# A held order of some 2000 operations made anew, with one copy and one product on other engines

## The chip, the cores and the metric

The kernel runs on one core of one Trainium2 chip. Its time is the device time of one execution in microseconds (us). Engines are named as the profile names them: PE is TensorE (PEld its weight loads), DVE is VectorE, ACT is ScalarE, POOL is GpSimd, SP is SyncE, which here only issues transfers and loads registers.

## The reference

Attention of 4 batches, 8 heads, 768 positions and 64 dimensions, with a sink of 4 positions and a window of 128, is followed by a mixture of experts in which each of the 3072 tokens goes to one of 8 experts:

```python
keep = (pos[None, :] < n_sink) | ((rel >= 0) & (rel < window))
scores = np.where(keep, q @ k.T / sqrt(D), -1e9)
a = np.exp(scores - scores.max(-1)); a /= a.sum(-1) + 1e-09
x = (a @ v) as (3072, 512)
e_idx = np.argmax(x @ w_gate, axis=1)
gate_w = softmax(x @ w_gate)[token, e_idx]
eom = sigmoid(x @ w_output_gate)
for e in range(8):
    out[e_idx == e] = gate_w * eom[:, e] * (np.maximum(x_e @ w1[e], 0) @ w2[e])
```

## The kernel before

**A planner.** The kernel does not issue its work as the loops come. Each operation is recorded with `pl.op(engine, duration, function, reads, writes, at=due time)`, and `Plan.order()` makes a list schedule from it: it steps through the five engines, starts on each the operation that can begin earliest by the assumed durations, and among those that can begin within a few tens of ns of it takes the one with the lowest due time. The order that comes out is then held on every engine. So a table of due times (`AT`), the assumed durations (`dve`, `act`, `gps`, literal numbers) and the assumed delays (`LAG`, `RATE`, `LAND`) decide, before anything runs, which operation stands behind which in each engine's queue.

**Attention** is 16 pairs of heads, 4 to a batch. `pair` issues for a pair: scaling q on POOL (L1060, three parts), scores on PE (L1076), fold of the window and row maximum on DVE (L1083 to L1088), exps on ACT (L1092), transposes of the exps on PE (L1112) in three groups j = 0, 1, 2, the copy of each group out of PSUM (ACT L1117, for j = 1 DVE L1119), masks of the copy on POOL (L281, tiles f and g), the product with v on PE (L1170, L1182), the gate's product (L1192), its copy lgT on ACT (L1196) and transposes (L1202), the weighing lw on DVE (L1206), and the division of the output by the sums, x, on DVE (L1235, after PE L1232). x is stored to a table xd in memory.

**Routing** follows a batch. `gate_route` takes maximum and chosen expert on DVE (L411 to L426), counts with small matmuls on PE (L442, L444), finds each token's place (L454 to L481), builds ohrow on DVE (L487) and three parts of rhs (L495, two on POOL and the third on DVE), and sorts with a product on PE (L507). After batches 1 and 2 `rank_experts` (L549 to L571) and `early_table` choose two experts each for the early slots 0 to 3. After batch 3 `final_table` (L653 to L740, DVE alone) picks 13 more slots, one after another, and after each four picks works out a chunk of token indices (L691 to L710, then L538 to L540).

**The experts** are 17 slots. A slot gathers tokens from xd by indirect transfers on POOL (L765, tile xg), transposes them on PE (L825) into a high part xh (ACT L828) and a low part xl (DVE L830), multiplies by w1 (m1, L944; slot 0 plain, L925) into two PSUM buffers named s, takes the relu as hh (ACT L856) and hl (DVE L859), multiplies by w2 (m2, L982), scales the result, y (ACT L838), by the factor sc that was copied out of the gathered row (ACT L848), and writes it by an indirect transfer on POOL (L841). Raw weights come in by SP (L797) into four buffers and are split into a high part (ACT L800) and a low part (DVE L804).

Of the kernel before, what the change touches and what calls it, by code (L numbers as in the profile page):

```python
# [18 lines left out]
P = 128  # L19
# [29 lines left out]
SLOT0, STEP, PLAIN = 172000, 20000, 1  # L49
# [13 lines left out]
class Plan:  # L63

    LAG = {"PE": 180, "ACT": 40, "DVE": 40, "POOL": 60, "SP": 0, "X": 0}
    NEAR = {"PE": 60, "ACT": 60, "DVE": 60, "POOL": 100, "SP": 100, "X": 0}
    SWITCH = {"row": 200}
    RATE, LAND = 0.35, 2000
# [18 lines left out]
    def op(self, eng, took, fn, r=(), w=(), at=0, busy=None, mode=None, size=0, behind=(), chain=None, hold=()):  # L87
# [23 lines left out]
        if isinstance(at, tuple):  # L111
            cls, at = at, at[0] + sum(AT[x] for x in at[1:])
        self.ops.append({"cls": cls, "eng": eng, "took": took, "busy": took if busy is None else busy, "fn": fn, "deps": deps - {i},
                         "uses": uses, "at": at, "mode": mode, "size": size, "chain": chain})
        return i

    def order(self):
# [13 lines left out]

        def room(fam, n):
# [11 lines left out]
        def start_of(i):  # L144
            o = ops[i]
            t = max(free[o["eng"]], earliest[i])
            if o["mode"] is not None and o["mode"] != mode:
                t += self.SWITCH.get(o["mode"], 150)
            elif o["mode"] is not None and t > free["PE"] + 50:
                t += 60  # L150
# [12 lines left out]
        while len(out) < len(ops):
            best = None
            for e, xs in ready.items():
# [3 lines left out]
                lim = min(ts)[0] + self.NEAR[e]  # L169
# [1342 lines left out]
```

## Time and profile before

| | |
|---|---|
| time, median of 3 runs | 607.68 us (604.41 to 612.07) |
| the profiled execution | 606.5 us; its span 604.7 us |
| granted TensorE clock, mean | 0.953 of full speed |
| busy: PE, DVE, ACT, POOL | 516.4, 357.1, 274.4, 190.9 us |
| attention and routing of three batches | 0 to about 230 us |
| slots 0 and 1, final table | about 230 to 290 us |
| the other slots | about 290 us to the end |

The three stretches overlap: an early slot is prepared while the last pairs run. PE holds most of the span, so the places where PE stands idle are what to look for, each with the instruction that ended it. A row of the timeline gives in brackets how long its engine was idle ahead of it, and what released it.

### The profile page before, as it was taken

The numbers are of one execution on the slowest core, as the hardware profiler recorded it, in microseconds if no ns is written. First come the engines' busy times: TensorE is split into PE (matmuls) and PEld (weight loads), VectorE is DVE, ScalarE is ACT, GpSimd is POOL, SyncE is SP. The second block draws the span as 40 slices with busy tenths as digits, with TensorE's granted clock in tenths as the row PEclk, the third lists the DMA queues.
The fourth block names the chain that finished last, engine by engine and source line by source line (L and its number), as shares of the span: only waits on it lengthen the run. The fifth ranks groups of instructions, "written<-read, shape, count | busy, mean of one in ns | idle before, by whom it ended". The sixth has DMA issues, their size and how long they took to land. (4 is left out here: it accounts for less than half of the span.)

```text
span 604.7 us, 10373 instructions
## 1 busy us (share of the span) xinstructions
PE 516.4 (85%) x3480; PEld 401.3 (66%) x3480; DVE 357.1 (59%) x822; ACT 274.4 (45%) x725; POOL 190.9 (32%) x292
## 2 busy tenths in 40 slices
PE   4999788888885997875888999999999698989992
PEld 2566555555554783664878788798777586677972
DVE  6776786598668644989762345435546344556420
ACT  4566566445753533434162434515535334356320
POOL 8467574766754410311112121121110302100110
PEclk9799999899998998979798999999999988999998
DMA  7354757389952376545653883636797717968540
GB/s 218 122 138 137 136 143 138 99 173 386 278 135 55 50 174 133 159 155 173 210 194 120 315 311 106 232 120 226 268 337 247 240 41 238 339 236 291 198 164 17
DMA packets 68959, 112.60 MB, mean 186 GB/s; under 512 B 8316, under 2 KB 35200, under 8 KB 68898
## 3 DMA queue, kind: packets, MB, share of 16 engines
q1 hardware_dynamic: 64434, 97.94, 53.5%
q0 software_dynamic: 4464, 13.91, 7.2%
q8 instruction: 30, 0.49, 0.4%
q14 instruction: 31, 0.25, 0.1%
HBM read 98.26 MB, written 13.25 MB: 184 GB/s over the span
## 5 line engine op out<-in xcount | busy, mean ns | idle before, releaser
L1092 ACT ACTIVATE e<-s,nmx 128x132 f32<-128x132 f32 x192 | 69.7, 371 | 56.1 <-DVE nmx L1088 39.9
L1076 PE MATMUL s<-k,q 64*128 64x260 f32 (+1 forms) x384 | 65.1, 431 | 13.2 <-ACT e L1092 6.5
L859 DVE SCALAR_TENSOR_TENSOR hl<-s,hh 128x512 fp32r<-128x512 f32 (+1 forms) x36 | 26.8, 749 | 71.9 <-ACT hh L856 71.9
L841 POOL DMA_INDIRECT out_dram<-y,idx x20 | 21.6, 1079 | 139.7 <-ACT y L838 104.8
L765 POOL DMA_INDIRECT xg<-xd,idx x21 | 22.9, 1091 | 130.0 <-PE tp L825 123.5
L1076 PEld LDWEIGHTS s<-k,q 64*128 64x128 f32 x384 | 34.0, 200 | 31.9 <-ACT e L1092 15.3
L856 ACT ACTIVATE hh<-s 128x512 fp32r<-128x512 f32 (+1 forms) x36 | 23.0, 644 | 68.0 <-PE s L944 66.0
L1085 DVE COPY_PREDICATED s<-maskf,s 128x256 f32<-128x256 int32 x80 | 33.8, 422 | 29.4 <-PE s L1076 25.8
L1060 POOL TENSOR_SCALAR q<-q 128x256 f32<-128x256 f32 x48 | 40.4, 856 | 11.4 <-DMA q<-in_qT_dram 9.0
L1088 DVE TENSOR_REDUCE nmx<-s 128x2 f32<-128x264 f32 x96 | 41.5, 432 | 3.3
L1092 ACT ACTIVATION_READ_ACCUMULATOR e<-s,nmx 128x1 f32 x192 | 38.7, 202 | 0.0
L1112 PE MATMUL tp<-ident,e 128*128 128x128 f32 x192 | 31.7, 291 | 4.2 <-DVE x L1235 2.4
L281 POOL TENSOR_SCALAR_AFFINE_SELECT g<-f 128x512 f32<-128x512 f32 (+1 forms) x48 | 28.4, 592 | 21.0 <-ACT f L1117 10.5
L1112 PEld LDWEIGHTS tp<-ident,e 128*128 128x128 f32 x192 | 21.6, 146 | 13.7 <-issue 3.5
L281 POOL TENSOR_SCALAR_AFFINE_SELECT f<-f 128x512 f32<-128x512 f32 (+1 forms) x48 | 28.6, 595 | 3.3
L830 DVE TENSOR_TENSOR xl<-tp,xh 128x512 fp32r<-128x512 f32 x23 | 15.4, 687 | 23.7 <-ACT xh L828 14.4
L1170 PE MATMUL oA<-f,v 128*64 128x128 f32 x256 | 26.7, 287 | 2.4 <-ACT e L1092 1.6
L838 ACT ACTIVATE y<-oA,sc 128x512 f32<-128x512 f32 (+1 forms) x18 | 11.7, 651 | 32.8 <-PE oA L982 27.2
L848 ACT COPY sc<-xg 128x1 f32<-128x1 f32 x28 | 5.0, 195 | 45.9 <-DMA xg<-xd,idx 28.2
L1235 DVE TENSOR_TENSOR x<-tp,rs 128x512 f32<-128x512 f32 (+1 forms) x32 | 17.6, 550 | 13.7 <-PE tp L1232 7.0
L1117 ACT COPY f<-tp 128x512 f32<-128x512 f32 x32 | 18.7, 586 | 13.3 <-PE tp L1112 12.9
L1232 PE MATMUL tp<-ident,ot 128*128 128x128 f32 x96 | 17.1, 289 | 7.7 <-DVE x L1235 5.6
(537 smaller groups left out, 1555.1 us busy)
## 6 DMA issues: line engine op xcount, KB each, us to landing
raw<-in_w_dram SPq DMA_DIRECT2D x96, 512.0 KB
v<-in_vx_dram SPq DMA_DIRECT2D x16, 384.0 KB
xd<-x SPq DMA_DIRECT2D x16, 384.0 KB
k<-in_kx_dram SPq DMA_DIRECT2D x15, 396.0 KB
q<-in_qT_dram SPq DMA_DIRECT2D x15, 384.0 KB
wa1h<-in_w_dram SPq DMA_DIRECT2D x5, 512.0 KB
wa1l<-in_w_dram SPq DMA_DIRECT2D x5, 512.0 KB
wa2h<-in_w_dram SPq DMA_DIRECT2D x3, 512.0 KB
```

The lines of the kernel that those rows point to most:

```text
L281: nc.gpsimd.affine_select(out=ap, in_=ap if src is None else src, pattern=pattern, compare_op=op, fill=fill, base=base, channel_multiplier=cm)
L765: nc.gpsimd.indirect_dma_start(out=p.get(key), out_offset=None, in_=xd[0:n + 1, :], in_offset=bass.IndirectOffsetOnAxis(ap=ids(), axis=0))
L841: nc.gpsimd.indirect_dma_start(out=where, out_offset=bass.IndirectOffsetOnAxis(ap=ids(), axis=0), in_=p.get(yk)[:, 0:m], in_offset=None, b ...
L856: nc.scalar.activation(out=p.get(hh)[:, :, 0:n], in_=p.get(ps)[:, :, 0:n], func=AF.Relu)
L859: nc.vector.scalar_tensor_tensor(out=p.get(hl)[:, :, 0:n], in0=p.get(ps)[:, :, 0:n], scalar=0.0, in1=p.get(hh)[:, :, 0:n].bitcast(F32), op ...
L1060: nc.gpsimd.tensor_scalar(out=c, in0=c, scalar1=SCALE, scalar2=None, op0=ALU.mult)
L1076: nc.tensor.matmul(out=get(s)[:, a, o0:P + CW], lhsT=get(q)[r, t * P:(t + 1) * P], rhs=get(k)[r, k0:k0 + P + CW - o0], start=True, stop=True)
L1085: nc.vector.copy_predicated(out=both[:, :, 4:CW], mask=bc(maski[:, 1, 4:CW], 1, 2), data=z[:, :, 0:P])
L1088: nc.vector.tensor_reduce(out=get(nmx)[:, t, :], in_=both, axis=AX.X, op=ALU.max, negate=True)
L1092: nc.scalar.activation(out=get(e)[:, t, a, :], in_=get(s)[:, a, P:P + CW], func=AF.Exp, bias=get(nmx)[:, t, a:a + 1], scale=1.0, accum_out ...
L1112: nc.tensor.transpose(out=get(tp)[:, i, :], in_=get(e)[:, 2 * j + i // 2, i % 2, 4:CW], identity=ident)
L1170: nc.tensor.matmul(out=o, lhsT=v_[:, kt, r], rhs=src[:, kt, a, :], start=t == kt == 0 or t == kt + 1 == 4, stop=False, skip_group_check=True)
```

## The change

It replaces the due times and the assumed durations and delays, and so the order on all five engines. Beside that it moves five things: the copies of group j = 1 go from DVE to ACT (16 instructions), the third part of rhs goes from DVE to POOL (4 instructions), the nine small sums that make `unit_of` on POOL become an operation of the plan, `final_table` gets a clock of due times of its own in place of the one that it shared with `gate_route`, and the first product of slot 0 is issued in two halves with other operations behind which it must stand. A cache in the planner makes it quicker and changes no order.

```diff
-SLOT0, STEP, PLAIN = 172000, 20000, 1
+SOFT = 1810
+SLOT0, STEP, PLAIN, FSTEP = 182180, 20000, 1, 800
 AT = {
-    "load": -15884, "v": 16617, "vs": 25612, "sinkv": 22184, "scale0": -9065, "scale1": -12038, "scale2": -3093,
+    "load": -19780, "v": 10768, "vs": 163198, "sinkv": -13952, "scale0": 28418, "scale1": -104693, "scale2": 64567,
...
-    LAG = {"PE": 180, "ACT": 40, "DVE": 40, "POOL": 60, "SP": 0, "X": 0}
+    LAG = {"PE": 260, "ACT": 60, "DVE": 80, "POOL": 55, "SP": 30, "X": 0}
-    RATE, LAND = 0.35, 2000
+    RATE, LAND = 0.39, 2200
...
-                lim = min(ts)[0] + self.NEAR[e]
+                t, i = min(ts)
+                lim = t + max(AT["near"] if e == "PE" else self.NEAR[e], ops[i]["soft"])
...
-def dve(n):
-    return {"took": 160 + 1.045 * n, "busy": 75 + 1.045 * n}
+def dve(n, k=1):
+    return {"took": k * 160 + 1.045 * n, "busy": k * 160 - 85 + 1.045 * n}
...
-                return p.op(eng, fn=fn, r=r, w=w, at=next(clock), **cost)
+                return p.op(eng, fn=fn, r=r, w=w, at=(next(clock), "rt"), **cost)
...
-            for q in (0, 2):
-                v(gps(512, 2.5), expand(nc.gpsimd, q), r=["oh2", "ohj"], w=[("rhs", q)], eng="POOL")
-            v(dve(768), e4, r=["jf"], w=["oh"])
-            v(dve(700), expand(nc.vector, 4), r=["oh2", "ohj"], w=[("rhs", 4)])
+            for q in (0, 2, 4):
+                v({"took": 1490, "busy": 1460}, expand(nc.gpsimd, q), r=["oh2", "ohj"], w=[("rhs", q)], eng="POOL")
+            v(dve(850), e4, r=["jf"], w=["oh"])
...
+        def units_of():
+            for q, z in enumerate(SIZES):
+                if z > 1:
+                    u = unit_of[:, q, 0:z // 2]
+                    nc.gpsimd.tensor_tensor(out=u, in0=u, in1=upp.broadcast_to([P, z // 2]), op=ALU.add)
+
+        pl.op("POOL", 1500, units_of, w=["unit_of"], at=60000)
...
-        def final_table(v):
+        def final_table(p):
+            clock = iter(range(SLOT0, SLOT0 + 1000 * FSTEP, FSTEP))
+            def v(cost, fn, r=(), w=()):
+                return p.op("DVE", fn=fn, r=r, w=w, at=(next(clock), "ft"), **cost)
...
-                    if j != 1:
-                        nc.scalar.copy(out=dst, in_=get(tp))
-                    else:
-                        nc.vector.tensor_copy(out=dst, in_=get(tp))
+                    nc.scalar.copy(out=get(f)[:, two].rearrange("p t a r -> p (t a) r"), in_=get(tp))
```

What the new order does is seen at three places. Names with a number are one buffer each.

DVE, at the end of the final table: the last steps of the table (`nrem`, `more_i`), the low part xl of slot 2's tokens and the low parts of its weights. Before:

```order
L737 TENSOR_REDUCE nrem<-rem 128x1
L738 CAST nrem_i<-nrem 128x1
L739 TENSOR_TENSOR nrem<-nrem,special 128x1
L740 CAST more_i<-nrem 128x1
L830 TENSOR_TENSOR xl_3498<-tp_3407,xh_3432 128x4x128
L830 TENSOR_TENSOR xl_3498<-tp_3419,xh_3432 128x4x128
L804 TENSOR_TENSOR wb2l<-raw_3371,wb2h 128x1024
```

Now the same xl (L867) stands between the sixth and the seventh pick, behind the table's first chunk (`idx`) alone:

```order
L747 SCALAR_TENSOR_TENSOR idx<-idx,upp 128x12
L713 SCALAR_TENSOR_TENSOR key<-units,less 128x8
L714 TENSOR_REDUCE top<-key 128x1
L715 TENSOR_SCALAR who<-key,top 128x8
L867 TENSOR_TENSOR xl_3384<-tp_3332,xh_3352 128x4x128
L719 SCALAR_TENSOR_TENSOR units<-who,units 128x8
L719 SCALAR_TENSOR_TENSOR less<-who,less 128x8
L719 SCALAR_TENSOR_TENSOR off<-who,off 128x8
L867 TENSOR_TENSOR xl_3384<-tp_3340,xh_3352 128x4x128
```

Slot 2's xl has moved from behind the table's four chunks to behind the first of them; the four hl of slot 1, which stood among the first chunks, now stand ahead of the first pick and behind the eight low parts of slot 1's weights (wc0l to wa3l), and the count of batch 3 on PE has moved from the middle of slot 0's second product to behind slot 1's first.

ACT, at the end of the last pair: the copies ot of its output, the factor sc of slot 3's first gather and the last pair's lgT. Before:

```order
L1186 COPY ot_2924<-oA 128x512
L1187 COPY ot_2924<-oB 128x256
L828 CAST xh_2896<-tp_2919 128x4x128
L848 COPY sc_2945<-xg_2889 128x1
L1196 COPY lgT_2954<-oB 96x256
L848 COPY sc_2973<-xg_2937 128x1
```

Now:

```order
L1216 COPY ot_2934<-oA 128x512
L1217 COPY ot_2934<-oB 128x256
L865 CAST xh_2892<-tp_2929 128x4x128
L1226 COPY lgT_2952<-oB 96x256
L885 COPY sc_2969<-xg_2885 128x1
```

lgT has moved ahead of the copy that waits for a gather.

DVE, routing of batch 2 with the ranks of the experts; x is the last output part of that batch but one. Before:

```order
L564 CAST order_i<-od 128x2
L568 COPY had<-taken 128x8
L570 TENSOR_TENSOR taken<-taken,perm 128x8 x2
L571 SCALAR_TENSOR_TENSOR base<-taken,base 128x8
L487 TENSOR_TENSOR ohrow<-io_101,jf 128x768
L495 TENSOR_TENSOR rhs<-oh_141,ohj 128x512
L1235 TENSOR_TENSOR x_2408<-tp_2580,rs_1883 128x256
```

Now that x (`x_2462`) and its weighing stand ahead of the ranks (`u`), and ohrow (L517) is followed by folds of scores (L1122, L1125) and the next pair's x:

```order
L1265 TENSOR_TENSOR x_2462<-tp_2496,rs_2048 128x256
L1236 TENSOR_TENSOR lw_2511<-tp_2491,rs_2048 128x192
L488 TENSOR_TENSOR pos<-pos,ohb 128x48
L489 TENSOR_REDUCE tokpos<-pos 128x6
L579 SCALAR_TENSOR_TENSOR u<-u,io_97 128x8
...
L517 TENSOR_TENSOR ohrow<-io_101,jf 128x768
L1122 COPY_PREDICATED s_2548<-maskf,s_2548 128x2x128
L1125 TENSOR_REDUCE nmx_2352<-s_2548 128x2
L1265 TENSOR_TENSOR x_2572<-tp_2559,rs_2226 128x512
```

The routing's steps have moved from one block to places between the pairs' own steps, and the third rhs is gone from DVE.

## Rows read from the trace of the kernel before

**Rows 1.** The page's first part: busy us of each engine, its share of the span, instructions.

```profile
PE 516.4 (85%) x3480; PEld 401.3 (66%) x3480; DVE 357.1 (59%) x822; ACT 274.4 (45%) x725; POOL 190.9 (32%) x292
```

**Rows 2.** The list of waits of PE, longest first: who waits for whom, us in total, times, longest us.

```profile
PE s L944 <- DVE hl L859: 15.3, 4, 5.9
PE s L944 <- DVE xl L830: 8.9, 2, 8.5
PE s L1076 <- ACT e L1092: 6.5, 11, 1.8
PE tp L1232 <- DVE x L1235: 5.6, 3, 4.8
```

**Rows 3.** PE's timeline: start, duration in us, instruction, count, and in brackets the idle time before it and its releaser. The two rows without brackets follow on the one above them at a few us.

```profile
4.79 1.68 PE L1076 MATMUL s<-k,q 64*128 64x260 f32 x8 [4.79 <-POOL q L1060]
107.27 0.70 PE L1170 MATMUL oB<-g,v 128*64 128x128 f32 x4 [3.87 <-POOL g L281]
194.32 1.12 PE L1232 MATMUL tp<-ident,ot 128*128 128x128 f32 x4 [4.75 <-DVE x L1235]
233.61 2.08 PE L982 MATMUL oB<-wa2h,hh 128*128 128x512 f32 x2 [3.85 <-ACT lgT L1196]
235.80 1.63 PE L982 MATMUL oA<-wa2h,hh 128*128 128x512 f32 x2
238.13 1.02 PE L982 MATMUL oA<-wa2l,hh 128*128 128x512 f32 x2
261.17 0.58 PE L944 MATMUL s<-xh,wb0h 128*128 128x256 f32 x1 [5.92 <-DVE hl L859]
290.24 0.58 PE L944 MATMUL s<-xl,wc3h 128*128 128x256 f32 x1 [8.46 <-DVE xl L830]
330.32 0.39 PE L944 MATMUL s<-xh,wb2h 128*128 128x256 f32 x1 [1.50 <-DVE hl L859]
484.62 0.58 PE L944 MATMUL s<-xh,wc0h 128*128 128x256 f32 x1 [5.48 <-DVE hl L859]
```

**Rows 4.** Busy time in stretches of 10 us: PE, PEld, DVE, ACT, POOL with their counts, then the granted clock, the DMA share and GB/s.

```profile
190.00:200.00 10.00, 5.68 (x36) 4.12 (x38) 7.48 (x18) 2.39 (x13) 3.73 (x6) 0.66 0.15 41
280.00:290.00 10.00, 0.89 (x6) 0.46 (x4) 9.27 (x46) 4.48 (x7) 4.61 (x4) 0.74 0.47 170
```

**Rows 5.** DVE's timeline around the final table: the first step after batch 3's count and the first pick, one of the low parts of weights and the pick behind it, the first chunk from its first step to a pick behind it, an hl of slot 1, xl of slot 2, and two hl of slot 2.

```profile
240.21 0.21 DVE L454 TENSOR_TENSOR pos<-tp,base 128x48 f32<-128x48 f32 x1 [0.56 <-PE tp L444]
243.68 0.16 DVE L676 SCALAR_TENSOR_TENSOR key<-units,less 128x8 f32<-128x8 f32 x1
...
252.04 1.22 DVE L804 TENSOR_TENSOR wc3l<-raw,wc3h 128x1024 fp32r<-128x1024 f32 x1
253.18 0.16 DVE L676 SCALAR_TENSOR_TENSOR key<-units,less 128x8 f32<-128x8 f32 x1
255.08 0.18 DVE L691 TENSOR_TENSOR selq<-who,io 128x32 f32<-128x32 f32 x1
259.89 0.16 DVE L676 SCALAR_TENSOR_TENSOR key<-units,less 128x8 f32<-128x8 f32 x1
260.43 0.68 DVE L859 SCALAR_TENSOR_TENSOR hl<-s,hh 128x512 fp32r<-128x512 f32 x1
288.90 1.28 DVE L830 TENSOR_TENSOR xl<-tp,xh 128x512 fp32r<-128x512 f32 x2
301.69 0.69 DVE L859 SCALAR_TENSOR_TENSOR hl<-s,hh 128x512 fp32r<-128x512 f32 x1 [2.15 <-ACT hh L856]
304.53 0.69 DVE L859 SCALAR_TENSOR_TENSOR hl<-s,hh 128x512 fp32r<-128x512 f32 x1 [2.15 <-ACT hh L856]
```

**Rows 6.** ACT's timeline: copies of sc that wait for a gather, and lgT behind the first of them.

```profile
233.10 0.19 ACT L848 COPY sc<-xg 128x1 f32<-128x1 f32 x1 [5.37 <-DMA xg<-xd,idx_e]
233.20 0.36 ACT L1196 COPY lgT<-oB 96x256 f32<-96x256 f32 x1
328.86 0.19 ACT L848 COPY sc<-xg 128x1 f32<-128x1 f32 x1 [5.13 <-DMA xg<-xd,idx]
483.16 0.19 ACT L848 COPY sc<-xg 128x1 f32<-128x1 f32 x1 [2.77 <-DMA xg<-xd,idx]
```

**Rows 7.** Groups of instructions by line, shapes kept apart: busy us, mean ns of one, idle before them; and the durations of rhs on both engines (minimum, median, maximum in ns).

```profile
L1060 POOL TENSOR_SCALAR q<-q 128x256 f32<-128x256 f32 x48 | 40.4, 856 | 11.4 <-DMA q<-in_qT_dram 9.0
L1117 ACT COPY f<-tp 128x512 f32<-128x512 f32 x32 | 18.7, 586 | 13.3 <-PE tp L1112 12.9
L1119 DVE COPY f<-tp 128x512 f32<-128x512 f32 x16 | 10.7, 670 | 0.0
L495 POOL TENSOR_TENSOR rhs<-oh,ohj x8: 1045/1488/1833, 76.4 to 244.8; 128x512 bf16<-128x512 bf16 x8
L495 DVE TENSOR_TENSOR rhs<-oh,ohj x4: 679/1528/1529, 77.1 to 245.7; 128x512 bf16<-128x512 bf16 x4
```

**Rows 8.** POOL's timeline: a scaling of q that waits for its transfer, with the mask behind it, the nine sums of `unit_of`, and the rhs of batch 2; DVE's timeline: one cast of the ranking in batch 2.

```profile
104.95 1.67 POOL L1060 TENSOR_SCALAR q<-q 128x256 f32<-128x256 f32 x2 [4.94 <-DMA q<-in_qT_dram]
6.34 1.38 POOL L599 TENSOR_TENSOR unit_of<-unit_of,upp 128x3 f32<-128x3 f32 x9
189.62 2.05 POOL L495 TENSOR_TENSOR rhs<-oh,ohj 128x512 bf16<-128x512 bf16 x2 [0.48 <-DVE od L563]
189.65 1.04 DVE L564 CAST order_i<-od 128x2 int32<-128x2 f32 x1
```

More of the change, by code (lines that the diff above doesn't have):

```diff
@@ L85, in get, with op @@
         return x["tile"]
-    def op(self, eng, took, fn, r=(), w=(), at=0, busy=None, mode=None, size=0, behind=(), chain=None, hold=()):
+    def op(self, eng, took, fn, r=(), w=(), at=0, busy=None, mode=None, size=0, behind=(), chain=None, hold=(), land=0, soft=0):
         i = len(self.ops)
@@ L130, in order @@
         end, earliest, out = {}, [0] * len(ops), []
+        stamp = dict.fromkeys(self.fam, 0)
+        opens = {}
+        for fam, xs in self.fam.items():
+            for b in xs:
+                if b["gate"] is not None:
+                    opens.setdefault(b["gate"], set()).add(fam)
+        cached = {}
         def room(fam, n):
@@ L142, in room, with buffers @@
             return xs[:n] if len(xs) >= n else None
[L144 to L150, printed above, removed]
+        def buffers(i):
             need = {}
-            for k in o["uses"]:
+            for k in ops[i]["uses"]:
                 x = self.inst[k]
@@ L920, in slot, with m1 @@
                     ps = new(p, "s", [P, 2, 512])
[L922 to L923 removed]
+                    for j in range(2):
+                        def m1(f0=f0, ps=ps, j=j):
                             for d in range(ND):
@@ L984, in slot @@
                     took = len(tiles) * (f32(512) if plain else 3 * f32r(512))
-                    p.op("PE", fn=m2, r=list(hs[f][0]) + [x for x in w2r[f][:2] if x], w=list(ys.values()), at=at + 11000 + f, **pe(took))
+                    p.op("PE", fn=m2, r=list(hs[f][0]) + [x for x in w2r[f][:2] if x], w=list(ys.values()), at=at + 11000 + f, behind=behind[1:], soft=SOFT if plain else 0, **pe(took))
                 for s in tiles:
@@ L1126, in trans @@
                 pl.op("PE", fn=go, r=[(e, 2 * j), (e, 2 * j + 1)], w=[tp], at=(at, "tr%d" % j), **pe(4 * TR))
-                if j != 1:
-                    pl.op("ACT", fn=copy, r=[tp], w=[(f, j)], at=(at, "tr%d" % j, "trc"), **act(512))
-                else:
-                    pl.op("DVE", fn=copy, r=[tp], w=[(f, j)], at=(at, "tr%d" % j, "trc"), **dve(512))
-                pl.op("POOL", fn=masks, r=[(f, j)], w=[(f, j), (g, j)], at=(at, "tr%d" % j, "mask"), took=n * 600 + 80, busy=n * 600)
+                pl.op("ACT", fn=copy, r=[tp], w=[(f, j)], at=(at, "tr%d" % j, "trc"), **act(512))
+                pl.op("POOL", fn=masks, r=[(f, j)], w=[(f, j), (g, j)], at=(at, "tr%d" % j, "mask"), took=n * 670, busy=n * 650)
             for j in range(3):
@@ L1206, in weigh @@
                 tt(out=get(lw), in0=lr.rearrange("p (t a e) -> p t a e", t=T, a=2), in1=bc(get(rs), 3, 2 * E), op=ALU.mult)
-            eng, name, cost = (nc.gpsimd, "POOL", gps(96)) if p < NP - 2 else (nc.vector, "DVE", dve(96))
+            eng, name, cost = (nc.gpsimd, "POOL", {"took": 390, "busy": 410}) if p < NP - 2 else (nc.vector, "DVE", dve(96))
             def add(a):
@@ L1266, in early @@
             load_reg(k, order_i[0:1, k:k + 1], ("order", r0), at - 14000)
-            slot(pl, k, 4, lambda j, s: idx_e[:, j, k, s:s + 1], ("idx_e", k), xds(done), done * S, at, plain=k < PLAIN, reg=lambda: regs[k], behind=pl.wrote[("s", NP - 1, T - 1)])
+            slot(pl, k, 4, lambda j, s: idx_e[:, j, k, s:s + 1], ("idx_e", k), xds(done), done * S, at, plain=k < PLAIN, reg=lambda: regs[k], behind=before if k == 0 else ())
         def xds(done):
```

132 lines of the change are left out of this document (75 added, 57 removed), and 6 rows, old and new, of the table AT.

## The prediction

> **What bounds the kernel now.** I read the page's first part before anything else: PE is busy for most of the span, no other engine for more than three fifths of it [rows 1]. So the work of PE sets a floor, and what an order can win is PE's idle time and the slow stretches that follow it. The chain of waits is followed back for a few per cent only, so I did not use it, and took the list of PE's waits [rows 2] and PE's timeline [rows 3] in its place. The reader is to see there that a few long waits carry most of it: hl and xl on DVE 24.2 us together, x on DVE 5.6, then lgT, a mask, and the start. Eleven waits for exps come to 6.5, so the short ones are about 0.6 each.
>
> Two things stand behind the long waits. Around the final table DVE is the bound: it is busy 9.27 of 10 us while PE is busy 0.89 [rows 4]. Elsewhere a queue's order is to blame: lgT ran at 233.20, directly behind a copy of sc that had waited 5.37 us for its gather [rows 6], and PE waited 3.85 for lgT [rows 3].
>
> A wait costs more than itself. In the 10 us from 190 the granted clock was 0.66 [rows 4], a mean that must hold stretches at the lower of TensorE's two levels (1.2 against 2.4 GHz). After the wait at 233.61 the next two entries took 2.08 and 1.63 us where the same two matmuls took 1.02 at 238.13 [rows 3]: 1.06 + 0.61 = 1.7 us lost behind a wait of 3.85.
>
> **The change, part by part,** against the profiled execution, 606.5 us (the median of three runs is 607.7, so 1.2 more). A wait that goes is counted at its length, and at 1.7 more where it is long and nothing else will hold PE there.
>
> *lgT of the last pair.* It moves ahead of the copy of sc that waits. Gain 3.85 + 1.7 = **-5.5**. Late next is the last weighing on DVE, which nothing holds. Bounds: -5.5, and 0 if PE then waits for ot instead.
>
> *Routing of batch 2.* DVE takes it as one block, and PE stands 4.75 us for the x behind it [rows 3]. The new order puts that x ahead of the ranks and folds between the steps. 4.75 + 1.7 = 6.45; I take **-6**, since a little of x's own time stays. Bounds -6.5 and 0.
>
> *The final table.* Today PE waits 5.92 for an hl of slot 1 that stands behind the first chunk, and 8.46 for slot 2's xl, which stands behind the whole table [rows 3, 5]; 14.4 together. In the new order count time 0 from the end of batch 3's count. DVE's items up to the end of xl, by pitches from row to row [rows 5]: small steps to the first pick 3.5 less one low part of a weight of 1.14 that stood among them, 2.4; slot 1's last hl 0.7; ohrow about 0.9; three low parts of weights 3.4; a pick 0.8 (between 253.18 and 255.08 lie one pick and one low part), five outside the chunk 3.9; the table's index steps about 0.9; one chunk with its pick 4.8; xl 1.2. Sum 18.2. PE in that time has slot 1's second product. A fourth of a first product is 2.84 (hl to hl in slot 2), a whole one 11.4, the second as many columns; with sort and transposes, some 2, PE is there at 13.4 and waits **4.8**. Two fourths later (23.9) it needs a free s buffer, which slot 2's first hl gives: two picks, three low parts, a chunk, a half pick and the hl are 1.6 + 3.4 + 4.8 + 0.5 + 0.7 = 11.0 on DVE, 29.2, so it waits **5.3** more. Together 10.1 against 14.4, and a short wait for xh goes with it: I take **-5**. Bounds: 0 (DVE's work is the same and only its place differs) and -14.4.
>
> *Copies of sc ahead of hh.* In slot 10 two sc that wait for gathers stand ahead of the first hh; the second ran at 483.16, and PE waited 5.48 [rows 3, 6]. Now the hh is first, and PE has one fourth more to do before it needs the next: **-2.8**. In slot 3 the same at 328.86 cost 1.50 [rows 3, 6] and is put behind the second hh: **-1.5**. From slot 5 on PE, POOL and SP stand nearly as before.
>
> *The start.* The nine sums of `unit_of` take 1.38 us [rows 8] and now stand ahead of the first scaling of q, for which PE waits 4.79 [rows 3]: **+1.4**, with no cover.
>
> *The mask at 107.* POOL's mask stood behind a scaling of q that waited 4.94 for its transfer, and PE 3.87 for the mask [rows 3, 8]. The new order still has scalings between masks; I count half, **-2**, bounds +3.9 and -3.9.
>
> *Copies of f.* Sixteen copies leave DVE, 10.7 us, and come to ACT, 16 x 0.586 = 9.4 [rows 7]. ACT has 45% of the span [rows 1], and a copy fits between its exps; cost 0. Without that cover it would be 9.4. What DVE has free shortens waits for x and folds: **-2** of the short ones, bounds 0 and -5.
>
> *The third rhs.* DVE needed 0.68 for it alone and 1.53 beside POOL's; POOL takes 1.49 [rows 7]. The sort gets it about 1.5 us later. In batch 3 it is done at about 3.7 + 4.5 = 8.2, and PE comes to the sort after six eighths of a product, 8.6: hidden. Batches 0 to 2 lie among pairs. Cost 0; uncovered, 4 x 1.5 = +6. The trace also shows that DVE pays for POOL's work: while two rhs ran on POOL from 189.62, a cast of two elements on DVE took 1.04 us [rows 8]. The Trainium skill, "GPSIMD Engine Reference", opening paragraphs and section 1, speaks against this part of the change: it calls GpSimd the wrong engine for plain elementwise work, about half as fast as VectorE, and says that the two share their access to SBUF when a VectorE instruction has two inputs there. The trace agrees on the speed (1.49 against 0.68). By that rule the move would relieve DVE of little and cost the sort chain its +6.
>
> *New waits.* The order was changed for all five engines, and some pair will wait where none did. The nearest rows are the eleven waits for exps, 0.6 each [rows 2]; eight new ones give **+5**. Bounds: 0, and three of the length seen for x, +14.
>
> Sum: -5.5 - 6 - 5 - 2.8 - 1.5 + 1.4 - 2 - 2 + 5 = -18.4. 606.5 - 18.4 = 588.1, and with the 1.2 between profile and median **589 us**.
>
> **The rivals.**
>
> *The waits only move.* DVE's work up to slot 3 is what it was, and each long wait was one of several nearly as late. Then the table gives 0, batch 2 gives half (-3), the sc copies nothing, and lgT -3.85; with +1.4 and +5 that is 606.5 - 0.5 + 1.2 = 607, and with a part of the forecast's gains some 600. For it: after the new xl the table still stands ahead of slot 2's hl. Against it: DVE had pauses of 2.15 us between slot 2's hl [rows 5], into which the rest of the table can go.
>
> *Everything fits better.* The short waits in attention go too (-5 more on exps and x), no new ones come (-5), and the mask's wait goes whole (-2): 589 - 12 = 577.
>
> *Slower: scalings of q that wait ahead of masks.* POOL takes a later pair's scaling as soon as the order says, also when its transfer is still under way, and the masks behind it hold PE: once before, 3.87 us at 107 [rows 3, 8]. If the new places (two scalings ahead of a pair's last mask in most pairs) meet a late transfer in n pairs, the cost is 3.9 n. From n = 5 the forecast's gain of 18.4 is gone; from n = 8 it is 589 + 31 = 620. Against it: all of POOL's waits for transfers of q came to 9.0 us before [rows 7], 4.94 of it in this one place.
>
> *The third rhs on POOL stretches DVE,* as the cast at 189.65 shows it [rows 8]: up to +6 on the sort chains: 595, or with two lost microseconds elsewhere 597. The 1.04 us cast speaks for it; that the routing now has folds between its steps, against.
>
> **How the numbers follow.** The forecast has 0.48 with 584 to 595, the better fit 0.18, waits that only move 0.19, the stretched DVE 0.08, the late scalings 0.07 (half of it over 2% slower). A measurement here can tell about 2% from no change, 12 us: below 595.5 is faster, above 619.8 slower. Faster: 0.48 + 0.18 + 0.04 of the stretched case, less 0.03 = 0.67. Slower: 0.05, with a little from cases not thought of 0.07. Same: 0.26. The range takes the better fit in to 574 and the moved waits to 607.
>
> **What would show it.** PE's first matmul at about 6.2; no wait of PE for lgT at slot 0's second product; no wait over 2 us for x in batch 2; two waits of some 5 us around slot 2's xl and first hl in place of 5.92 and 8.46; at slot 10 a wait under 3; DVE's busy time down by 10 to 16, ACT's up by 9, POOL's by 6; PE's own busy time down by a few us through less time at the lower clock. The prediction is wrong in its core if PE's idle time around the table stays at 14 us or more, if masks or q appear among PE's longest waits, or if the list shows many new waits of 1 to 2 us in attention.

## The result and the profile after

The changed kernel takes 589.89 us (median of 4 runs, 587.8 to 592.25) against 607.36 us of the kernel before on the same chip: a ratio of 0.971, 95% interval 0.963 to 0.978, faster. The forecast was 589. The profiled execution took 590.1 us, its span is 588.2. All medians leave out executions in a second, slower state: one of h_front's (971.59 us, the other five lie between 594.2 and 602.0), one of h_back's, and a few of the kernel before in the later sessions.

The page's first part of the changed kernel, and PE's list of waits (us in total, times, longest):

```profile
PE 519.1 (88%) x3480; PEld 402.6 (68%) x3480; DVE 346.5 (59%) x802; ACT 280.7 (48%) x741; POOL 193.9 (33%) x296
```

```profile
PE s L981 <- DVE hl L896: 8.8, 6, 3.6
PE s L981 <- DVE xl L867: 6.5, 2, 4.5
PE s L1113 <- POOL q L1097: 6.2, 1, 6.2
PE s L1113 <- ACT e L1129: 6.2, 7, 2.7
PE tp L1175 <- POOL pk L1169: 5.1, 3, 3.3
PE oB L1200 <- POOL g L311: 4.5, 3, 2.5
PE s L981 <- ACT xh L865: 3.4, 2, 2.5
PE tp L472 <- DVE ohb L449: 2.8, 1, 2.8
```

PE stood 604.7 - 516.4 = 88.3 us of the span before [rows 1] and 588.2 - 519.1 = 69.1 now: 19.2 less. Its busy time rose by 2.7 with the same number of instructions, so 16.5 are left. Against [rows 2], hl went from 15.3 to 8.8, xl from 8.9 to 6.5, and x and lgT are gone from the top. New are POOL's pk, ohb behind POOL's logits, and xh. The masks g stand in the list as before (4.8 then, one of 3.87 and a short one; 4.5 now, in three).

PE's timeline of the changed kernel, the rows that answer to [rows 3]:

```profile
6.25 1.68 PE L1113 MATMUL s<-k,q 64*128 64x260 f32 x8 [6.25 <-POOL q L1097]
...
46.66 0.69 PE L1200 MATMUL oB<-g,v 128*64 128x128 f32 x4 [2.50 <-POOL g L311]
71.58 0.20 PE L472 MATMUL tp<-ohb,upper 128*128 128x48 bf16 x1 [2.84 <-DVE ohb L449]
120.42 0.44 PE L1200 MATMUL oB<-g,v 128*64 128x128 f32 x4 [1.78 <-POOL g L311]
138.56 2.06 PE L1113 MATMUL s<-k,q 64*128 64x260 f32 x8 [2.73 <-ACT e L1129]
164.34 0.40 PE L1175 MATMUL tp<-ident,pk 128*40 128x128 f32 x1 [3.29 <-POOL pk L1169]
...
268.06 0.38 PE L981 MATMUL s<-xh,wc3h 128*128 128x256 f32 x1 [2.54 <-ACT xh L865]
272.94 0.58 PE L981 MATMUL s<-xl,wc3h 128*128 128x256 f32 x1 [4.49 <-DVE xl L867]
283.84 0.39 PE L981 MATMUL s<-xh,wc3h 128*128 128x256 f32 x1 [2.46 <-DVE hl L896]
473.91 0.58 PE L981 MATMUL s<-xh,wc0h 128*128 128x256 f32 x1 [3.59 <-DVE hl L896]
```

The wait of 3.87 for a mask at 107 is gone, and four waits for POOL's work of 1.8 to 3.3 us, 10.4 together, stand in attention in its place (ohb at 71.58 is DVE's, and DVE waits there for POOL's lg). POOL's timeline at the first, the third and the fourth of them tells why:

```profile
44.35 0.85 POOL L1097 TENSOR_SCALAR q<-q 128x256 f32<-128x256 f32 x1 [3.44 <-DMA q<-in_qT_dram]
45.17 0.85 POOL L1246 TENSOR_TENSOR lg<-lg,lw 128x96 f32<-128x96 f32 x2
45.97 0.64 POOL L311 TENSOR_SCALAR_AFFINE_SELECT g<-f 128x512 f32<-128x512 f32 x1
...
116.47 1.67 POOL L1097 TENSOR_SCALAR q<-q 128x256 f32<-128x256 f32 x2 [4.57 <-DMA q<-in_qT_dram]
...
160.81 1.68 POOL L1097 TENSOR_SCALAR q<-q 128x256 f32<-128x256 f32 x2 [4.01 <-PE s L1113]
```

A scaling of a later pair's q waits for its transfer, and the sums of logits, masks and packing that PE needs next wait behind it. The second place has the same form: a scaling at 67.20 waited 2.10, lg stands behind it, and DVE waited 2.68 for lg. At the fourth the profile names PE, the last reader of the buffer, as the releaser; whether it or the transfer held the scaling is open. All of POOL's waits for transfers of q came to 16.0 us, against 9.0 before [rows 7].

The fifth new wait, 2.73 for exps at 138.56, has another cause. Batch 1's routing is still one block on DVE, from pos at 131.60 to order_i at 135.98, and the folds and row maxima for those exps stand behind it. That the routing's steps were moved between the pairs' own steps holds for batch 2, not for batch 1.

Each of the four waits for POOL's work has a low clock around it; in the kernel before, the same stretches show 1.00. The windows (columns as in [rows 4]):

```profile
40.00:50.00 10.00, 7.39 (x67) 5.36 (x65) 4.02 (x12) 3.86 (x18) 5.27 (x9) 0.83 0.36 103
70.00:80.00 10.00, 8.42 (x61) 6.19 (x61) 8.45 (x32) 5.24 (x23) 4.12 (x9) 0.66 0.34 91
120.00:130.00 10.00, 9.31 (x53) 5.71 (x55) 6.83 (x22) 5.95 (x24) 6.86 (x12) 0.66 0.43 117
160.00:170.00 10.00, 6.40 (x43) 4.66 (x40) 2.90 (x10) 2.74 (x11) 8.13 (x12) 0.66 1.05 368
```

To place gains, this table (worked out from the starts in the timelines) gives the lead over the kernel before, in us, at four points: the last pair's lw on DVE (236.05 us in the kernel before) and three writes of results on POOL (282.11, 346.58, 594.79). The lower rows are kernels of the experiments. Each row is one execution. In two of the experiments' executions the time was off by 2.3 and 3.8 us ahead of every operation that had been moved, so differences of under 3 us in this table tell nothing by themselves.

| profiled execution | last lw | slot 1's first write | slot 3's first write | last write |
|---|---|---|---|---|
| the changed kernel | 9.3 | 15.4 | 14.7 | 16.5 |
| h_front | 8.3 | 3.6 | 2.7 | 5.7 |
| h_back | 0.0 | 7.6 | 5.8 | 7.4 |
| a_q | 17.5 | 22.3 | 19.8 | 25.3 |
| a_best | 22.6 | 28.4 | 24.8 | 34.6 |
| a_best_tab | 21.1 | 29.1 | 15.8 | 25.1 |

### The profile page after: what moved, and what is told of

It is laid out like the page before. It is cut to its first block, busy times and chain, and to the rows that moved or that the text cites. A ratio compares the mean times of both kernels' runs of the same rounds, so it can differ in the third digit from the quotient of the medians.

```text
span 588.2 us, 10368 instructions
## 1 busy us (share of the span) xinstructions
PE 519.1 (88%) x3480; PEld 402.6 (68%) x3480; DVE 346.5 (59%) x802; ACT 280.7 (48%) x741; POOL 193.9 (33%) x296
## 5 line engine op out<-in xcount | busy, mean ns | idle before, releaser
L1113 PE MATMUL s<-k,q 64*128 64x260 f32 (+1 forms) x384 | 69.6, 442 | 12.9 <-POOL q L1097 6.2
L1113 PEld LDWEIGHTS s<-k,q 64*128 64x128 f32 x384 | 37.4, 205 | 29.5 <-ACT e L1129 14.3
L1122 DVE COPY_PREDICATED s<-maskf,s 128x256 f32<-128x256 int32 x80 | 33.9, 424 | 28.0 <-PE s L1113 24.0
L1125 DVE TENSOR_REDUCE nmx<-s 128x2 f32<-128x264 f32 x96 | 41.5, 432 | 3.3
L311 POOL TENSOR_SCALAR_AFFINE_SELECT g<-f 128x512 f32<-128x512 f32 (+1 forms) x48 | 27.1, 565 | 23.5 <-ACT f L1152 23.3
L1149 PE MATMUL tp<-ident,e 128*128 128x128 f32 x192 | 33.0, 301 | 1.8 <-DVE lw L1236 1.0
L1152 ACT COPY f<-tp 128x512 f32<-128x512 f32 x48 | 28.1, 588 | 13.1 <-PE tp L1149 12.6
L875 ACT ACTIVATE y<-oA,sc 128x512 f32<-128x512 f32 (+1 forms) x18 | 11.7, 651 | 41.0 <-PE oA L1019 34.6
L867 DVE TENSOR_TENSOR xl<-tp,xh 128x512 fp32r<-128x512 f32 x23 | 15.5, 686 | 26.2 <-ACT xh L865 26.2
L1149 PEld LDWEIGHTS tp<-ident,e 128*128 128x128 f32 x192 | 23.5, 153 | 10.0 <-issue 3.7
L311 POOL TENSOR_SCALAR_AFFINE_SELECT f<-f 128x512 f32<-128x512 f32 (+1 forms) x48 | 26.9, 561 | 3.3
L878 POOL DMA_INDIRECT out_dram<-y,idx_e x8 | 9.7, 1214 | 49.1 <-ACT y L875 24.5
L1265 DVE TENSOR_TENSOR x<-tp,rs 128x512 f32<-128x512 f32 (+1 forms) x32 | 17.5, 550 | 13.8 <-PE tp L1262 13.7
L862 PE MATMUL tp<-ident,xg 128*128 128x128 f32 (+1 forms) x112 | 16.0, 271 | 4.2 <-ACT hr L935 2.5
```

The source lines that it names most:

```text
L311: nc.gpsimd.affine_select(out=ap, in_=ap if src is None else src, pattern=pattern, compare_op=op, fill=fill, base=base, channel_multiplier=cm)
L878: nc.gpsimd.indirect_dma_start(out=where, out_offset=bass.IndirectOffsetOnAxis(ap=ids(), axis=0), in_=p.get(yk)[:, 0:m], in_offset=None, b ...
L1113: nc.tensor.matmul(out=get(s)[:, a, o0:P + CW], lhsT=get(q)[r, t * P:(t + 1) * P], rhs=get(k)[r, k0:k0 + P + CW - o0], start=True, stop=True)
L1122: nc.vector.copy_predicated(out=both[:, :, 4:CW], mask=bc(maski[:, 1, 4:CW], 1, 2), data=z[:, :, 0:P])
L1125: nc.vector.tensor_reduce(out=get(nmx)[:, t, :], in_=both, axis=AX.X, op=ALU.max, negate=True)
L1149: nc.tensor.transpose(out=get(tp)[:, i, :], in_=get(e)[:, 2 * j + i // 2, i % 2, 4:CW], identity=ident)
```

## The experiments

Most kernels here keep all operations and move a few in an engine's list. For that the held order is taken apart by engine, and `MOVES` names what goes ahead of what: `("ACT", 217, 216)` puts the operation at place 217 of ACT's list ahead of the one at 216. The lists are merged again so that every operation stands behind what it needs.

```diff
-        for _, i in self.order():
+        for i in self.moved([i for _, i in self.order()]):
             self.ops[i]["fn"]()
```

### The order before, mended by hand at three places

The theory: a few places carry the gain, so mending them in the old order brings most of it. One kernel mends lgT, one the final table, one the routing of batch 2, one all three.

```diff
+    MOVES = (("ACT", 217, 216), ("PE", 350, 349))
```

> The order of the kernel before, with two operations moved by hand: the last pair's lgT ahead of the sc that waits for slot 3's gather (ACT), and its transposes ahead of slot 0's second product (PE). Theory (the gain comes from a few places in the order): PE's wait of 3.85 us at 233.61 goes with the 1.7 us at the lower clock behind it, and the end comes 5 us earlier, 602. Rival (the waits only move): the 3.85 goes, the wait for hl at 261 grows by as much, since DVE's final table sets that place, and the time stays within 2 us of before.

```diff
+    MOVES = (("DVE", 372, 356), ("DVE", 373, 356), ("DVE", 378, 366), ("DVE", 380, 375))
```

> The order of the kernel before, with four operations of DVE moved by hand: slot 2's xl from behind the final table to the middle of its third chunk, and the first two hl of slot 2 ahead of low parts of weights that stood before them. Theory: the wait of 8.46 us falls to under 2, the rest of the table goes into DVE's pauses in slot 2, and the end comes 5 to 7 us earlier, 601. Rival (the waits only move): 8.46 goes, and a wait for slot 2's hl or slot 3's xl of 5 us or more comes in its place; no change within 2 us.

```diff
+    MOVES = (("DVE", 239, 233), ("DVE", 240, 236), ("DVE", 244, 237), ("DVE", 245, 237),
+             ("PE", 310, 309), ("PE", 311, 309), ("PE", 312, 309), ("PE", 313, 309),
+             ("PE", 314, 309), ("PE", 315, 309), ("PE", 316, 309), ("PE", 317, 309))
```

> The order of the kernel before, with batch 2's routing loosened by hand: the x and the copy of f that stood behind it go between its steps, two folds go ahead of ohrow, and on PE the scores and products of the next pair go ahead of the sort. Theory: the wait of 4.75 us at 194 falls to about 1 and the clock does not fall there; the end comes 3 to 5 us earlier, 603. Rival: PE then waits at the sort or at a mask for most of it; within 2 us of before.

> The three moves by hand together, 18 of some 2000 operations, no engine changed. Theory (the three places are most of the gain, and they add): 5 + 6 + 4 = 15 us, 592, within 5 us of the changed kernel. Rival (the gain is spread over the whole order, or comes from the copies and the rhs that changed engine): no more than 5 us, 602 or above.

Against 609.00 us of the kernel before in the same session: lgT 609.15 (ratio 1.000, 0.996 to 1.004), routing 609.88 (1.002, 0.998 to 1.007), the table 619.15 (1.016, 1.006 to 1.026), all three 614.6 (1.013, 1.004 to 1.021). No gain anywhere; the theory fell. The table and all three came out slower than either of their two expectations. With lgT mended, PE waited for none, but its timeline has this:

```profile
245.65 0.39 PE L543 MATMUL tp<-rhs,ohrow 128*128 128x256 bf16 x2 [2.55 <-DVE ohrow L523]
...
261.08 0.58 PE L980 MATMUL s<-xh,wb0h 128*128 128x256 f32 x1 [4.62 <-DVE hl L895]
```

It comes to the same matmul of slot 1 at 261.08, as at 261.17 before [rows 3]. The next late thing was again on ACT: a second copy of sc waits for its gather, batch 3's exps dd stand behind it, and on DVE den, which needs dd, stands ahead of pos and with it of the whole sort and table:

```profile
238.87 0.19 ACT L884 COPY sc<-xg 128x1 f32<-128x1 f32 x1 [4.56 <-DMA xg<-xd,idx_e]
238.97 0.24 ACT L465 ACTIVATE dd<-dd 128x48 f32<-128x48 f32 x1
```

```profile
239.24 0.20 DVE L503 TENSOR_REDUCE den<-dd 128x6 f32<-128x48 f32 x1 [5.61 <-ACT dd L465]
...
240.06 0.17 DVE L490 TENSOR_TENSOR pos<-tp,base 128x48 f32<-128x48 f32 x1
```

DVE started pos at 240.21 before [rows 5], so lgT's 3.85 us turned into DVE's 5.61. In the changed kernel one sc, not two, stands ahead of dd, and pos comes at 252.58 with three of slot 1's hl ahead of it, so that PE has work until the table is ready.

With the routing mended, PE no longer waits for x at that place, but 8 us later for a weighing on DVE:

```profile
202.53 0.69 PE L1268 MATMUL tp<-ident,ot 128*128 128x128 f32 x2 [2.71 <-DVE lw L1242]
```

The low clock came along: 0.66 from 200 to 210, where it had been 0.66 from 190 to 200 [rows 4]. The last pair's lw starts at 235.76, against 236.05 before, so 0.3 is left of the 4.75. Here the next late thing is on the same engine.

With the table mended, the wait of 8.46 for xl shrinks to 0.74, but a low part of weights, wb2l, slips from 290.10 to 301.34 us. Most of that comes from the hl that was put ahead of it: it waited 4.99 us on DVE for its hh, which stood on ACT behind a copy of sc that waited 5.82 us for a gather (296.58). (The execution was also 3.8 us late at the last lw, ahead of everything that was moved.) There are four buffers for raw weights, and the low part is the last reader of one. DVE's, ACT's and PE's timelines of that kernel:

```profile
301.34 1.22 DVE L840 TENSOR_TENSOR wb2l<-raw,wb2h 128x1024 fp32r<-128x1024 f32 x1
```

```profile
306.73 1.04 ACT L836 CAST wc2h<-raw 128x1024 fp32r<-128x1024 f32 x1 [9.47 <-DMA raw<-in_w_dram]
307.69 1.08 ACT L892 ACTIVATE hh<-s 128x512 fp32r<-128x512 f32 x2
```

```profile
298.04 0.58 PE L980 MATMUL s<-xh,wc3h 128*128 128x256 f32 x1 [4.10 <-DVE hl L895]
...
309.05 0.58 PE L980 MATMUL s<-xh,wc3h 128*128 128x256 f32 x1 [6.54 <-DVE hl L895]
```

PE stands 4.10 us for the hl that waited. The next load starts when that buffer is free, its cast waits 9.47 us on ACT, two hh of slot 2 stand behind the cast, and PE stands 6.54 for the hl made from them.

### Order or engines

The new theory has two forms: the order as a whole carries the gain, or the work taken from DVE does. Two kernels cross them: the old order with the two moves between engines, and the new order without them.

```diff
-                    if j != 1:
-                        nc.scalar.copy(out=dst, in_=get(tp))
-                    else:
-                        nc.vector.tensor_copy(out=dst, in_=get(tp))
+                    nc.scalar.copy(out=dst, in_=get(tp))
...
-                v(dve(700), expand(nc.vector, 4), r=["oh2", "ohj"], w=[("rhs", 4)])
+                v(dve(700), expand(nc.gpsimd, 4), r=["oh2", "ohj"], w=[("rhs", 4)])
```

> The kernel before with its held order untouched, and only the two moves between engines made in it: every transposes' copy on ScalarE, the third sort operand on GpSimd. Theory A, the new order carries the gain and the two moves only go along with it: same, 605 to 611 us. Rival B, VectorE paces the stage up to the final table (it was its waits that came back when three of them were taken out by hand) and the work taken from it is the gain: 9 to 13 us faster, 595 to 599 us.

The second undoes both in the changed kernel.

> The changed kernel with its new held order untouched, and the two moves undone: the middle group's copies back on VectorE, the third sort operand back on VectorE. Theory A (the order carries the gain): at most 3 us lost, 588 to 593 us. Rival B (the work taken from VectorE carries it): 9 us or more lost, 599 us or more. Both at once would show as 593 to 599.

The old order with the moves: 609.38 us against 608.71 (1.001, 0.997 to 1.005). The new order without them: 592.66 (0.977, 0.970 to 0.984). The order carries the gain. The moves give at most a few us in the new order, and the two intervals against the kernel before (0.963 to 0.978 with them) overlap, so that is not told from nothing.

### Which half of the order

Each operation of the changed kernel was matched with its place in the old order, and two kernels hold a list made of both (`HELD`, the numbers of all operations), cut at the last pair's lw. The planner then may start only the head of each engine's list.

```diff
+        for i in HELD:
+            lanes.setdefault(ops[i]["eng"], []).append(i)
...
+            for e, xs in lanes.items():
+                if not xs or missing[xs[0]]:
+                    continue
+                t, i = start_of(xs[0]), xs[0]
```

> The changed kernel, its engines and its operations, with a held order made of two: up to the last block's scaling of the logits (lw, where the changed kernel is 9.3 us ahead of the kernel before) each engine's list is the new one; everything behind it follows in the order before. If the gain of the front part is its own and stays, and the back part's is its own too: 598 to 600 us, ahead by 9 us at that scaling and by 9 us at the end. If the front's lead is lost again to what is late behind it (as the lead of the three places mended by hand was): 604 us or more, ahead by 9 us there and by less than 4 at the first write.

> The other half: up to the last block's scaling of the logits each engine's list is that of the kernel before, everything behind it follows in the new order. If the two parts add: 599 to 601 us, level with the kernel before at that scaling, 6 us ahead at slot 1's first write and 7 to 8 us at the end. If the back part can use its order only with the front's lead (its operations wait for transfers that the front starts): 604 us or more.

New front, old back: 600.50 us (ratio 0.983, 0.977 to 0.989). Old front, new back: 597.22 (0.979, 0.974 to 0.985). Against 608.15 that is 7.7 and 10.9 us, 18.6 together, and the whole change gave 17.5. So by the times the halves add, as far as they tell: each of the two is uncertain by 3 to 4 us, and both are built on the changed kernel, so that its moves between engines and its start at 6.25 count twice. The traces qualify it. At the last write the leads of the halves come to 5.7 + 7.4 = 13.1 of the 16.5, and the new front's lead of 8.3 at lw fell to 3.6 at slot 1's first write, as the expectation of a lost lead had it, while the time lies nearer the other expectation. The old back has its waits of [rows 3] as before, here in PE's timeline of h_front, and then of h_back:

```profile
256.67 0.58 PE L1071 MATMUL s<-xh,wb0h 128*128 128x256 f32 x1 [5.67 <-DVE hl L986]
286.63 0.58 PE L1071 MATMUL s<-xl,wc3h 128*128 128x256 f32 x1 [8.37 <-DVE xl L957]
```

```profile
275.88 0.58 PE L1071 MATMUL s<-xh,wc3h 128*128 128x256 f32 x1 [2.43 <-ACT xh L955]
280.87 0.58 PE L1071 MATMUL s<-xl,wc3h 128*128 128x256 f32 x1 [4.40 <-DVE xl L957]
```

### One priced place, undone in the new order

```diff
+    MOVES = (("ACT", 233, 232), ("PE", 354, 353))
```

> The changed kernel with the one operation back that the prediction priced at 5.5 us: the last block's copy of the logits behind the scaling of slot 3 on ScalarE. If this place is worth its price in the new order: 594 to 596 us, with a wait of 3 to 4 us for the copy on TensorE. If the waits only move, as they did when it was mended in the order before: at most 1.5 us lost, 588 to 591.5 us, and the wait at the first scaled tile of slot 2's stage shorter by what the new one takes.

Measured: 598.13 us (0.980, 0.974 to 0.987), with five runs at 592.2, 592.8, 598.1, 598.4 and 599.3; the expected 594 to 596 lies between the groups, which a_back shows too (591.8 to 592.7, and 597.7 and 598.6). The time alone settles little; the trace is clearer. PE's timeline, from the last pair's pack to slot 2's first product:

```profile
201.25 0.29 PE L1211 MATMUL tp<-ident,pk 128*40 128x128 f32 x1 [1.39 <-POOL pk L1205]
228.49 2.07 PE L1055 MATMUL oB<-wa2h,hh 128*128 128x512 f32 x2 [3.88 <-ACT lgT L1262]
270.60 0.38 PE L1017 MATMUL s<-xh,wc3h 128*128 128x256 f32 x1 [2.46 <-ACT xh L901]
```

69.35 us, where the changed kernel takes 64.48 (203.58 to 268.06): 4.9 lost behind a wait of 3.88. Counted from the same pack, 4.4 are still lost at the last write. The same place was worth nothing in the old order.

### The late scalings, and a version that beats both

```diff
+    MOVES = (("POOL", 32, 31), ("POOL", 33, 31), ("POOL", 34, 31), ("POOL", 53, 51), ("POOL", 54, 51), ("POOL", 55, 51),
+             ("POOL", 95, 93), ("POOL", 96, 93), ("POOL", 98, 93), ("POOL", 130, 127), ("POOL", 131, 127), ("POOL", 132, 127))
```

> The changed kernel with GpSimd's logit adds, masks, guards and packing put ahead of the scalings of q that wait for a late transfer, at the four places where TensorE waits for GpSimd now (46, 71, 120 and 164 us of its span). If those waits and the lower granted clock behind them lie on the path: 5 to 10 us faster than the changed kernel, 580 to 585 us. If the stage is paced by another engine and the waits only move: within 2 us of it, 588 to 592 us.

582.22 us (0.956, 0.951 to 0.962), as expected if the waits lie on the path. Its lead at lw is 17.5 in place of 9.3, so the four waits had cost at least 8.2 there. POOL's waits for transfers of q are down to 3.9 us. In the windows three of the four places have the clock back (the fourth, from 150 to 160, shows 0.84, with a new wait in it), and the page's first part shows what PE's busy time became:

```profile
40.00:50.00 10.00, 9.65 (x98) 6.89 (x97) 6.93 (x20) 7.33 (x31) 7.42 (x14) 1.00 0.87 192
62.00:72.00 10.00, 8.88 (x99) 6.33 (x95) 9.44 (x33) 6.46 (x28) 6.26 (x11) 1.00 0.63 174
112.00:122.00 10.00, 7.87 (x80) 5.02 (x78) 8.63 (x31) 7.10 (x31) 7.67 (x14) 1.00 0.65 134
```

```profile
PE 512.4 (88%) x3480; PEld 399.6 (69%) x3480; DVE 347.2 (60%) x802; ACT 280.6 (48%) x741; POOL 193.9 (33%) x296
```

The span went from 588.2 to 579.4 us, 8.8 less. PE's idle time fell by only 2.1 of them (69.1 to 67.0), its busy time by 6.7 for the same instructions: most of the gain is clock.

The idle time fell by so little because new waits appeared, 4.91 for psk and one of 2.32 at 158.90:

```profile
148.03 0.41 PE L1248 MATMUL oA<-psk,vst 64*128 64x384 f32 x1 [4.91 <-DMA psk<-hlk]
```

SP had issued six weight loads of 512 KB in the 4.8 us ahead of the three sends of psk (20 KB each). The next kernel keeps the twelve moves and adds eight (the table of unit numbers, two loads and one raw load behind the sends, slot 10's relu):

```diff
+             ("POOL", 0, 4), ("SP", 95, 93), ("SP", 96, 93), ("SP", 97, 93),
+             ("SP", 107, 106), ("SP", 108, 106), ("SP", 109, 106), ("ACT", 387, 385),
```

> The changed kernel with GpSimd's list mended at the four places as before (582.2 us), and three more: the table of unit numbers behind the first scalings of q, two of slot 1's weight loads and one raw load behind the sends of psk that they hold up (TensorE waits 4.9 and 2.3 us for psk there), and slot 10's relu ahead of the casts that hold it up. If each of these waits lies on the path: 1.4 + 3.5 + 1 + 2 less, 574 to 576 us. If the waits only move: 580 us or more.

574.81 us (0.945, 0.941 to 0.949): the start is at 4.79 again, of psk's waits one of 1.94 is left, slot 10's is gone. That the loads held up the sends is argued from the order and from this wait; the eight moves were made together, and none of them was run alone.

The last one mends the final table too, by hand:

```diff
+             ("DVE", 293, 336), ("DVE", 295, 336), ("DVE", 317, 336), ("DVE", 319, 336), ("DVE", 321, 347),
+             ("DVE", 337, 347), ("DVE", 339, 347), ("DVE", 367, 347), ("DVE", 368, 347), ("ACT", 255, 260),
+             ("ACT", 260, 266), ("ACT", 261, 266), ("ACT", 265, 263), ("ACT", 269, 260), ("ACT", 270, 266),
```

> The kernel of the last run (574.8 us) with the final table mended as well: on VectorE the table's steps (the selected token numbers and the index chunks) ahead of weight chunks that nobody waits for yet, on ScalarE the casts of slot 1's rows and the scaling ahead of the weight casts that wait for late raw loads. TensorE waits there for xh 2.5, xl 4.5 and hl 3.7 us. If these waits lie on the path as their places in the changed kernel suggest: 5 to 8 us faster, 567 to 570 us. If the waits only move (as they did in the order before, where the same kind of edit cost 10 us): 574 us or more.

584.37 us against 608.39 there (0.958, 0.953 to 0.962): slower than without. The waits for xh and hl at the table shrank (2.54 to 0.87 and 3.65 to 0.64), and slot 1 was written 0.7 us earlier. The wait for xl stayed (4.29), one of 3.50 for xh came at 288.57, and then came this, in PE's timeline, and on ACT and DVE ahead of it:

```profile
310.20 0.58 PE L1017 MATMUL s<-xh,wb2h 128*128 128x256 f32 x1 [13.47 <-DVE hl L932]
```

```profile
301.93 1.04 ACT L873 CAST wa3h<-raw 128x1024 fp32r<-128x1024 f32 x1 [13.41 <-DMA raw<-in_w_dram]
...
308.20 0.59 ACT L929 ACTIVATE hh<-s 128x512 fp32r<-128x512 f32 x1
```

```profile
296.62 1.22 DVE L877 TENSOR_TENSOR wa2l<-raw,wa2h 128x1024 fp32r<-128x1024 f32 x1
```

The low part wa2l, last reader of a raw buffer, ran at 287.75 without the edit, and wa3h was cast at 292.52. It is the mechanism of the hand-mended table once more: a low part that "nobody waits for yet" holds a buffer, and the casts of the next loads stand ahead of hh on ACT.

## Why the prediction was right, step by step

The time and the side came out, and on either side of the last lw nearly the sums: forecast terms up to it were -9.1 (lgT -5.5, routing -6, start +1.4, mask -2, f -2, new waits +5), measured -9.3; what came behind was forecast at -9.3 and measured at 16.5 - 9.3 = 7.2 in the profiled pair. The agreement up to lw is luck in part. The mask and the new waits were forecast at +3 and came to +4.3 or more; what is left for the routing and the copies, about -10 where -8 was forecast, is a remainder that no run measured. Of the forecast's own signs of being wrong, one came true by its wording: q (6.2, which is the start, as forecast) and masks (4.5) stand among PE's longest waits. The masks already did so before, so the sign could not tell. Single steps did less well.

| step | forecast | measured |
|---|---|---|
| start | +1.4 | +1.5 (6.25 against 4.79); undone in a_best, 4.79 |
| lgT | -5.5 | -4.9 in the new order, 0 in the old |
| routing of batch 2 | -6 | x wait of 4.75 gone; 0 in the old order; not undone in the new, so its size there is not shown |
| mask at 107 and new waits | -2 + 5 | -3.9 and at least +8.2 |
| copies of f, third rhs | -2, 0 | together +0.7 (old order) and -2.8 (new), not told from 0 |
| final table | -5 | -5.4 from lw to slot 3's first write, with slot 3's sc in it; h_back alone -5.8 there |
| sc, slots 3 and 10 | -1.5, -2.8 | waits 1.50 to 0.31, 5.48 to 3.59: -1.2, -1.9 |

**The table.** Two waits of 4.8 for xl and 5.3 for hl were worked out; they are 4.49 and 2.46, and ahead of them stands one of 2.54 for xh that I had said would go. It is ACT's: the cast wa1h waits 7.99 us for a raw load at 264.83, with y and the xh behind it. The sum (9.5 against 10.1) came out, the division did not. On DVE the items up to the end of xl took 20.3 us (252.58 to 272.88) where 18.2 had been added up: ohrow took 1.81, a key 1.00 and a who 0.78 beside POOL's rhs, where they take 0.95, 0.16 and 0.23 by themselves, and that is 2.3 of it. The wait for hl is shorter because PE needed 8.4 us for the two fourths ahead of it, not 5.7, with a granted clock of 0.50 from 273 to 278. (Of the eight low parts of weights that stand ahead of slot 1's hl, five, wc3l to wc5l, wa2l and wa3l, are slot 2's.)

**The new waits.** They were counted as eight of 0.6 by the rows for exps. Four are of 1.8 to 3.3, by the mechanism of the rival with late scalings, with n = 4; at 3.9 each it would have been 15.6, they cost at least 8.2. A fifth, of 2.73, is the routing's of batch 1. That step was mis-sized, and with it the forecast that PE's busy time would fall: it rose by 2.7. With the scalings put behind, PE's busy time is 512.4 us for the same 3480 instructions, 6.7 below 519.1, as the clock of the windows above would have it.

**Slot 10.** PE waited 3.59, not 2.7: the copies of sc still wait 6.11 us on ACT ahead of the next hh. Mended in a_best, the lead grew by 7.9 us between the writes that were at 468.16 and 506.14 us before, on either side of this wait; in a_q by 3.3.

**The rival "the waits only move".** It was given 0.19 and did not come true for the change. But it is exactly what the old order does when one place is mended, and for a reason the forecast hadn't: at each place something else is late by nearly as much, a second engine's list (ACT's at lgT and at the table) or the next item on the same one (DVE's lw at the routing). My prices, read from PE's waits one by one, bought nothing as single moves in the old order. In the new order only lgT's was undone by itself, and there it held: 4.9 for 5.5.

**DVE stretched by the third rhs.** It did not show in the time. The rival's price was up to 6 us on the sort chains; undoing both moves brought no gain (592.66 against 589.89), and PE waits for no rhs. In batch 3 the third rhs stretched one more step (the who of 0.78; 0.23 in a_back) and took its own 0.68 off DVE. The Trainium skill, "GPSIMD Engine Reference", section 1, says that GpSimd shares its interface to SBUF with VectorE, and that VectorE instructions with two SBUF inputs contend for it. The trace agrees, with ohrow at 1.81 us beside a rhs.

Busy time moved the forecast way, but less: DVE -10.6 (10 to 16), ACT +6.3 (9), POOL +3.0 (6). POOL's is explained: with no rhs left on DVE, one takes 1.05 us on POOL (median of twelve). The 1.49 of [rows 7] was measured beside DVE's own, so the comparison of 1.49 with 0.68 in the prediction made POOL look slower than it is here; 1.05 against 0.68 is the fair pair.

## What to carry to other kernels

A long wait on the bounding engine is worth its length only if the next-late thing at that place is earlier by as much: read the releaser's own list, what it waits for, and what comes next there, before pricing a single move; if several things are late together, plan all of them anew with measured durations. After that, look at the heads of the queues: an instruction that waits for a transfer, with small urgent work behind it, was worth 7.7 us here in twelve moves, and eight more gave 7.4. Whoever postpones the last reader of a staging buffer postpones the load behind it, and a cast of that load at the head of another queue passes the delay on.

## What the runs showed of the hardware

Short waits cost clock as well: the four of 10.4 us together stand in windows with a granted clock of 0.66 to 0.83, and with the scalings put behind PE was busy 6.7 us less for the same instructions. A transfer of 20 KB was late behind six loads of 512 KB that the same queue had been given just before it: 4.91 us of PE's time, gone when two of the loads were put behind it, with other moves at the same time (1.94 is left at the next such place).

A rhs on POOL holds up an instruction of DVE that begins just behind it. The ohrow of DVE takes 0.94 to 0.95 us by itself. Here are POOL's and DVE's timelines of the changed kernel in batch 0, and DVE's in batch 3, where POOL's rhs began at 256.28:

```profile
80.23 1.05 POOL L525 TENSOR_TENSOR rhs<-oh,ohj 128x512 bf16<-128x512 bf16 x1
80.94 1.15 DVE L517 TENSOR_TENSOR ohrow<-io,jf 128x768 bf16<-128x768 f32 x1
...
256.34 1.81 DVE L517 TENSOR_TENSOR ohrow<-io,jf 128x768 bf16<-128x768 f32 x1
```

It began 0.71 and 0.06 us behind the rhs, and in a_back 0.58 behind one and took 1.28. In all three it ended 1.86 to 1.87 us behind the start of the rhs, as if it had done its work from 0.92 on. The cast of two elements in [rows 8], 0.03 behind the start of a rhs, took 1.04 and ended at 1.07. What begins first goes first: at 134.92, 0.01 us ahead of a rhs, ohrow took 0.94, and that rhs 1.85. In the kernel before it began 1 us into the first of POOL's rhs and took 0.95. A row maximum (nmx, at 80.40, one input) took its usual 0.43 beside the same rhs.
